# Re-pacing a convolution with a token search beside it: fewer search steps in one product stage, more in the last stage, and the input blocks dealt out anew

## The chip, the cores and the metric

One core of one Trainium2 chip runs the whole program. The metric is the device time of one launch in microseconds (us), the median of three runs. TensorE is called PE here, VectorE DVE, ScalarE ACT, GpSimd POOL and SyncE SP, as in the profile.

## The reference, cut to what matters

```python
def _attn_ref(x, h):                       # x (8, 6336, 128), h (6336, 128)
    L = 2 * S
    Yf = np.fft.rfft(x, n=L, axis=1) * np.fft.rfft(h, n=L, axis=0)[None]
    return np.fft.irfft(Yf, n=L, axis=1)[:, :S, :]

def _moe_ref(x, w_gate, w1, w2, capacity): # capacity 128, w1 (128, 1024), w2 (1024, 128)
    scores = np.einsum('bsd,d->bs', x, w_gate)
    out = x.copy()
    for b in range(B):
        top_idx = np.argpartition(-scores[b], capacity)[:capacity]
        xe = x[b, top_idx]
        ye = np.maximum(xe @ w1, 0.0) @ w2
        g = 1.0 / (1.0 + np.exp(-scores[b, top_idx]))
        out[b, top_idx] = x[b, top_idx] + g[:, None] * ye
    return out
```

A long causal convolution along the sequence, for 8 batches and 128 channels, and then, per batch, the 128 tokens with the highest score pass through a small two-layer network, whose result is added to them.

## The kernel before, in words

The convolution is a Fourier transform of length 6336 = 99 x 64, cut into matrix products. Batches go in pairs: group g handles batches 2g and 2g+1 (`xb[0]` and `xb[1]`, called the first and the second input), and there are four groups. Before group 0 the filter h takes the same way once. A group has these stages, all written out by one Python program whose order is the order on every engine's queue:

- `stage_a` (line 143), the first transform. A block is 8 channels of one input. POOL turns the block (`turn`, line 137, tile `xt`, three buffers; a block's turn is issued two blocks ahead), PE multiplies it with the table `fa` (line 156), and ACT or DVE empties the PSUM bank into `yp` (lines 59 and 61). A block has two steps; a step is 8 products, which are 16 records in the trace. A group has 32 blocks: for each half u of the channels (u = 0, 1) eight of the first and eight of the second input. Here `blocks(i, u)` stands for the eight blocks of input i in half u.
- `stage_b` (line 189), the product with the filter's spectrum for one half u of the channels, in 25 chunks of frequencies. Per chunk SP loads a table `w` (256 KB, four buffers, so four chunks ahead) and a spectrum piece `hr` (256 KB, seven ahead), PE makes the second transform (line 198), ACT writes a negated and swapped copy into a second bank (lines 201 and 202), DVE multiplies twice (line 206), and POOL, or in the first half DVE for each fifth chunk, adds (line 213).
- `stage_c` (line 217), the first inverse transform of one half, 32 steps of PE and an emptying each, written to `zp`.
- `stage_d` (line 227), the last stage, 32 steps. Per step PE makes four products (line 239, 8 records in the trace), ACT copies to `hr` (line 243, four places in rotation), ACT's queue stores to the output, POOL multiplies by the gate weights (line 247, tile `tm`), DVE sums them to scores (line 249).

Beside the stages of group g runs the *side*, the selection and the network for the pair before (`moe`, line 429). It is a Python generator whose steps are dealt out between steps of the stages by `mix` (line 439): a rate of 0.4 means that after each main step 0.4 is owed, and a side step is issued whenever a whole one is owed. Its steps: 1 starts the keys, 4 to 11 and 12 to 19 are two searches for the threshold, each of eight comparisons (DVE compares and counts, lines 278 and 281; in the next step PE sums over the partitions, line 284, and DVE makes the next thresholds, lines 285 to 292); 20 to 28 turn the winners into row numbers (step 27 makes the `lane` tiles of the second batch on DVE, lines 353 and 355, and step 28 multiplies them on PE, lines 361 and 363); 29 issues two gathers on POOL (line 385); 32 to 36 and 37 to 41 are the network of the first and of the second batch (`feed`, line 391), each ended by a scatter on POOL (line 422) that waits for DVE's line 421; the last scatter is in step 42. The side of the last pair follows the last stage with nothing beside it.

In groups 1 to 3 `stage_a` is split: `part` (20 blocks, 40 steps) runs alone with the side, `more` (12 blocks) runs beside the first half's `stage_b`, one step after each chunk. The second half's `stage_b` then starts with four chunks alone, and after that the first half's `stage_c` is mixed in at 1.33 steps a chunk. `zp` lies over part of `xb[1]` and of `yp`, so that the second input of the next pair can be loaded only when the last stage has read `zp`; its load is issued behind the last stage (line 512), that of the first input at the start of the second half's `stage_c` (line 501).

Of the kernel before, what the change touches and what calls it, by code (L numbers as in the profile page):

```python
# [32 lines left out]
def conv_moe(ctx, tc, x, h, w_gate, w1, w2, fa_d, wb_d, wc_d, at_d, tri_d, cst_d, out):  # L33
# [10 lines left out]
    def bank():  # L44
        return pp_.tile([128, 512], F32, tag="p", name="p")
# [4 lines left out]
    def product(out, table, moving, start=True, stop=True):  # L50

        n = out.shape[0]
        for a in range(0, n, 64):
            b = min(a + 64, n)
            nc.tensor.matmul(out[a:b], table[:, a:b], moving, start=start, stop=stop)  # L55

    def empty(act, dst, src):
        if act:
            nc.scalar.copy(out=dst, in_=src)  # L59
        else:  # L60
            v.tensor_copy(out=dst, in_=src)  # L61
# [13 lines left out]
    def load_x(src, half, parts=range(0, N2, 16)):  # L75
        s = src.rearrange("(a c) d -> a c d", c=N2)
        for n0 in parts:
            nc.sync.dma_start(out=xb[half][:, n0:n0 + 16], in_=s[:, n0:n0 + 16])
# [25 lines left out]
    def ahead(key, only=None):  # L104

        i = tables.index(key)
        while loaded[0] < len(tables) and loaded[0] <= i + AHEAD:
            item = tables[loaded[0]]
            if only and item[1] != key[1]:
                break  # L110
            loaded[0] += 1
            wt = tp.tile([128, 512], F32, tag="w", name="w", bufs=AHEAD + 1)
            if item[0] == "at":
                have[item] = wt[0:N1, 0:4 * N1].rearrange("p (m c n) -> p m c n", m=2, c=2)
                nc.sync.dma_start(out=have[item], in_=at_d[:, item[2]:item[2] + 2])
                continue
            k0, kn = kchunks[item[3]]
            have[item] = wt.rearrange("p (k c) -> p k c", c=128)
            nc.sync.dma_start(out=have[item][:, 0:kn], in_=wb_d[:, k0:k0 + kn])
        if key not in spectra:  # L120
            return
        i = spectra.index(key)
        while loaded[1] < len(spectra) and loaded[1] <= i + DEEP:
            item = spectra[loaded[1]]
            if item[1] != key[1]:
                break
            ht = hr[:, loaded[1] % 8 * 512:loaded[1] % 8 * 512 + 512].rearrange("p (t k d) -> p t k d", t=2, d=HD)
            loaded[1] += 1
            k0, kn = kchunks[item[3]]
            nc.sync.dma_start(out=ht[:, :, 0:kn], in_=hd[:, item[2], item[3], :, 0:kn])  # L130
            have["h", item] = ht
# [5 lines left out]
    def turn(block):  # L137
        half, d0, _ = block
        xt = tp.tile([N1, 8, N2], F32, tag="xt", name="xt", bufs=3)
        nc.gpsimd.tensor_copy(out=xt.rearrange("p d n -> p n d"), in_=xb[half][:, :, d0:d0 + 8])  # L140
        turned[block] = xt

    def stage_a(blocks, acts, lead=()):


        todo = list(blocks) + list(lead)
        for i, block in enumerate(blocks):
            for b in todo[i:i + 3]:
                if b not in turned:
                    turn(b)  # L150
            xt = turned[block]
            for q in range(2):
                pt = bank()
                for j in range(4):
                    for c in range(2):
                        nc.tensor.matmul(pt[c * 64:(c + 1) * 64, j * N1:(j + 1) * N1], xt[:, q * 4 + j],  # L156
                                         fa[:, c * N1:(c + 1) * N1], start=True, stop=True)
                p0 = (block[2] + q * 4) // 2
                empty(acts[(2 * i + q) % len(acts)], yp[:, p0:p0 + 2].rearrange("p j k t -> p j t k"),
                      pt[:, 0:4 * N1].rearrange("p (j t k) -> p j t k", j=2, t=2))  # L160
                if q:
                    del turned[block]
                yield

    def row(k, c0, n):
        return yp[:, c0 // 2:(c0 + n) // 2, k]
# [22 lines left out]
    def stage_b(g, u, adds):  # L189

        c0 = u * D
        for ci, (k0, kn) in enumerate(kchunks):
            key = ("b", g, u, ci)
            ahead(key)
            wt, ht = have.pop(key), have.pop(("h", key))
            pt = bank()
            for j in range(kn):
                product(pt[:, j * D:(j + 1) * D], wt[:, j], row(k0 + j, c0, D))
            pv = pt[:, 0:kn * D].rearrange("p (k b) -> p k b", b=D)
            pw = bank()[:, 0:kn * D].rearrange("p (k b) -> p k b", b=D)  # L200
            nc.scalar.mul(out=pw[0:64], in_=pv[64:128], mul=-1.0)  # L201
            nc.scalar.copy(out=pw[64:128], in_=pv[0:64])  # L202
            yv = yp[:, c0 // 2:(c0 + D) // 2, k0:k0 + kn].rearrange("p j k t -> p k j t")

            def times(dst, src, t):
                v.tensor_tensor(out=dst, in0=src.rearrange("p k (b j t) -> p k b j t", b=2, t=2),  # L206
                                in1=ht[:, t, 0:kn].rearrange("p k (j t) -> p k j t", t=2).unsqueeze(2).broadcast_to(
                                    [128, kn, 2, HD // 2, 2]), op=ALU.mult)

            times(yv.rearrange("p k (b j) t -> p k b j t", b=2), pv, 0)  # L210
            tx = tp.tile([128, KC, D], F32, tag="t", name="tx", bufs=3)[:, 0:kn]
            times(tx.rearrange("p k (b j t) -> p k b j t", b=2, t=2), pw, 1)
            (v if adds[ci % len(adds)] else nc.gpsimd).tensor_tensor(  # L213
                out=yv, in0=yv, in1=tx.rearrange("p k (j t) -> p k j t", t=2), op=ALU.add)
            yield

    def stage_c(u, acts):

        for j0 in range(u * D, u * D + D, 4):
            pt = bank()  # L220
            for i in range(4):
                product(pt[0:N1, i * 128:(i + 1) * 128], yp[:, (j0 + i) // 2, :, i % 2], wc)
            empty(acts[j0 // 4 % len(acts)], zp[:, j0 // 2:j0 // 2 + 2].rearrange("p j m t -> p j t m"),
                  pt[0:N1].rearrange("p (j t m) -> p j t m", j=2, t=2))
            yield
# [213 lines left out]
    def mix(main, *others):  # L439


        owed = [0.0] * len(others)
        for _ in main:
            for i, (it, rate) in enumerate(others):
                owed[i] += rate
                while owed[i] >= 1:
                    owed[i] -= 1
                    next(it, None)

    def rest(it):  # L450
        for _ in it:
            pass

    def blocks(half, u, lo=0, hi=8):
        return [(half, u * HD + i * 8, u * D + half * HD + i * 8) for i in range(lo, hi)]
# [14 lines left out]
    hs, a = stage_h(), stage_a(blocks(0, 0), (1, 0), blocks(1, 0)[0:2])  # L470
# [7 lines left out]
    side = iter(())  # L478
    for g in range(G):
        last = g == G - 1  # L480
        if g:
            part = blocks(0, 0) + blocks(0, 1, 0, 4) + blocks(1, 0)
            more = blocks(0, 1, 4) + blocks(1, 1)
            mix(stage_a(part, (1,), more[0:2]), (side, 0.45 if last else 0.25))
        else:
            more = blocks(0, 1) + blocks(1, 1)
        a = stage_a(more, (1, 1, 1, 0))
        mix(stage_b(g, 0, (0, 0, 0, 0, 1)), (a, 2 * len(more) / 24))
        rest(a)
        b, c = stage_b(g, 1, (0,)), stage_c(0, (1, 1, 0))  # L490
        for _ in range(4):
            next(b)
        mix(b, (c, 1.33), (side, 0.4))
        rest(c)
        if not last:
            if g == 0:
                nc.sync.dma_start(out=w1s, in_=w1)
                nc.sync.dma_start(out=w2s, in_=w2.rearrange("(c p) d -> p c d", p=128))
                v.tensor_copy(out=upper16, in_=upper)
                v.tensor_copy(out=lane16, in_=cst[:, 0:1])  # L500
            load_x(x[2 * g + 2], 0)
        mix(stage_c(1, (1,)), (side, 0.36))
        ss = mp.tile([N1, 2, N2], F32, tag="sc", name="sc", bufs=2)
        d = stage_d(g, ss)
        mix(itertools.islice(d, 24), (side, 0.35))
        if not last:
            for bl in blocks(0, 0)[0:2]:
                turn(bl)
        mix(d, (side, 0.35))
        rest(side)  # L510
        if not last:
            load_x(x[2 * g + 3], 1)
            ahead(("b", g + 1, 0, 0))
        side = moe(2 * g, 2, ss, shared)
        next(side)
# [56 lines left out]
```

## Time and profile before

| | us |
|---|---|
| median of three runs | 1062.93 |
| the three runs | 1063.11, 1054.4, 1062.93 |
| the profiled execution | 1058.81 |
| its span in the trace | 1057.0 |
| mean granted TensorE clock | 0.96 of full speed |

Times in the trace count from the start of the span. A stage's share is read by the time at which PE begins it: group 0 multiplies the first half from 110.2, group 1 starts at 296.2, group 2 at 529.1, group 3 at 758.0; PE ends the last stage of group 3 near 992 and the span ends at 1057.0.

### The profile page before, as it was taken

Reading aid. Unit: us, or ns where it says so; the run is one execution under the profiler, and the core shown is the slowest. Engines: PE = TensorE matmul, PEld = TensorE weight load, DVE = VectorE, ACT = ScalarE, POOL = GpSimd, SP = SyncE. Lnnn points to the kernel's source line nnn. Section 1 sums busy time; section 2 is a strip of 40 time slices with the busy share of each in tenths; the row PEclk is TensorE's granted clock in tenths of the full one; section 3 lists DMA queues with packets and bytes.
Section 4 is the critical chain, followed back from the end, with each engine's and each line's share of the span. In section 5 each row is a group of like instructions: output and inputs, shape, how many; then the busy total and the mean of one; then the engine's idle time right before and its main releaser. Section 6 shows DMA issues by size and latency. Waiting matters only on the chain.

```text
span 1057.0 us, 33223 instructions
## 1 busy us (share of the span) xinstructions
PE 933.4 (88%) x13756; PEld 851.5 (81%) x13756; DVE 629.8 (60%) x1225; ACT 593.7 (56%) x1071; POOL 569.0 (54%) x472
## 2 busy tenths in 40 slices
PE   2968999999989988999999899999989999999505
PEld 2968989997779988987799888977778899977404
DVE  0467687703365989524368999323577998123573
ACT  1456787773356876653368776643447777643101
POOL 2504796605866965226777765046856865046401
PEclk9988999999998999999999999999989999999856
DMA  8798888625674986416576875246645984036300
GB/s 275 260 341 305 260 279 267 203 118 155 211 236 135 322 291 189 143 50 197 169 244 223 291 256 172 93 119 180 207 150 180 305 292 132 7 116 190 113 1 10
DMA packets 117003, 203.17 MB, mean 192 GB/s; under 512 B 11303, under 2 KB 54538, under 8 KB 113290
## 3 DMA queue, kind: packets, MB, share of 16 engines
q1 hardware_dynamic: 89590, 174.05, 50.6%
q10 hardware_dynamic: 26752, 25.96, 7.5%
q8 instruction: 109, 1.79, 0.7%
q0 software_dynamic: 512, 1.05, 0.4%
q14 instruction: 40, 0.33, 0.1%
HBM read 161.56 MB, written 39.45 MB: 190 GB/s over the span
## 4 chain that ended last, share of the span: by engine, by line
PE 62%; DVE 13%; DMA 9%; POOL 5%; issue 5%; ACT 4%; SPq 1%; POOLq 0%; DVEq 0%; ACTq 0%
PE p L55 30%; PE p L239 16%; PE p L156 12%; POOL tm L247 3%; DVE tx L206 2%; DMA w<-tab_wb 2%; DVE cmp L278 2%; DVE slots L206 2%; DMA hr<-hd 2%; DVE num L281 2%; DMA slots<-in_h 1%; DMA out<-hr 1%; DMA hd<-hr 1%; ACT p L201 1%; DVE thr L292 1%
## 5 line engine op out<-in xcount | busy, mean ns | idle before, releaser
L59 ACT COPY slots<-p 128x396 f32<-128x396 f32 (+1 forms) x446 | 261.4, 587 | 148.0 <-PE p L156 78.1
L213 POOL TENSOR_TENSOR slots<-slots,tx 128x512 f32<-128x512 f32 x180 | 233.1, 1311 | 123.8 <-DVE tx L206 82.0
L156 PE MATMUL p<-fa,xt 99*64 99x99 f32 x4608 | 235.7, 256 | 32.5 <-POOL xt L140 23.3
L156 PEld LDWEIGHTS p<-fa,xt 99*64 99x64 f32 x4608 | 220.6, 141 | 38.0 <-POOL xt L140 26.3
L55 PE MATMUL p<-wc,slots 128*64 128x128 f32 (+1 forms) x4096 | 243.6, 273 | 5.4 <-DVE tx L206 2.2
L55 PE MATMUL p<-slots,w 128*64 128x128 f32 x3168 | 221.2, 279 | 15.2 <-ACT p L202 4.0
L55 PEld LDWEIGHTS p<-wc,slots 128*64 128x64 f32 (+1 forms) x4096 | 226.3, 126 | 10.0 <-DVE tx L206 3.6
L239 PE MATMUL p<-slots,w 99*99 99x256 f32 x1024 | 225.6, 377 | 2.9 <-ACT slots L59 2.9
L247 POOL TENSOR_TENSOR tm<-hr,wg 99x512 f32<-99x512 f32 x128 | 161.9, 1273 | 113.6 <-ACT hr L243 110.8
L140 POOL COPY xt<-slots 99x512 f32<-99x512 f32 x144 | 166.0, 1175 | 105.5 <-PE p L156 65.3
L239 PEld LDWEIGHTS p<-slots,w 99*99 99x99 f32 x1024 | 165.6, 163 | 57.0 <-ACT slots L59 3.8
L249 DVE TENSOR_REDUCE sc<-tm 99x4 f32<-99x512 f32 x128 | 87.9, 686 | 199.1 <-POOL tm L247 199.1
L55 PEld LDWEIGHTS p<-slots,w 128*64 128x64 f32 x3168 | 187.1, 136 | 19.5 <-ACT p L202 7.6
L206 DVE TENSOR_TENSOR slots<-p,hr 128x512 f32<-128x512 f32 (+1 forms) x200 | 136.1, 681 | 46.1 <-ACT p L202 45.7
L243 ACT COPY hr<-p 99x512 f32<-99x512 f32 x128 | 75.0, 586 | 139.0 <-PE p L239 125.9
L201 ACT ACTIVATE p<-p 64x512 f32<-64x512 f32 (+1 forms) x200 | 113.1, 566 | 67.3 <-PE p L55 57.7
L206 DVE TENSOR_TENSOR tx<-p,hr 128x512 f32<-128x512 f32 (+1 forms) x200 | 135.0, 675 | 0.0
L202 ACT COPY p<-p 64x512 f32<-64x512 f32 (+1 forms) x200 | 110.8, 554 | 6.3
L61 DVE COPY slots<-p 128x396 f32<-128x396 f32 (+1 forms) x98 | 60.0, 615 | 42.5 <-PE p L156 40.9
L385 POOL DMA_INDIRECT xe<-out,iu x8 | 8.0, 996 | 103.1 <-DVE cmp L353 88.3
L55 PE MATMUL m<-num,ones 99*35 99x6 bf16 (+1 forms) x128 | 14.1, 184 | 44.8 <-DVE num L281 44.7
L55 PEld LDWEIGHTS <-ones 99*35 99x35 bf16 (+1 forms) x128 | 8.9, 108 | 50.4 <-DVE num L281 42.6
(85 smaller groups left out, 453.5 us busy)
## 6 DMA issues: line engine op xcount, KB each, us to landing
w<-tab_wb SPq DMA_DIRECT2D x192, 256.0 KB
hr<-hd SPq DMA_DIRECT2D x192, 256.0 KB
slots<-in_x SPq DMA_DIRECT2D x32, 792.0 KB
out<-hr ACTq DMA_DIRECT2D x128, 198.0 KB
w<-tab_at SPq DMA_DIRECT2D x128, 153.1 KB
slots<-tab_wb SPq DMA_DIRECT2D x24, 256.0 KB
hd<-hr SPq DMA_DIRECT2D x24, 256.0 KB
slots<-in_h SPq DMA_DIRECT2D x4, 792.0 KB
```

The lines of the kernel that those rows point to most:

```text
L55: nc.tensor.matmul(out[a:b], table[:, a:b], moving, start=start, stop=stop)
L59: nc.scalar.copy(out=dst, in_=src)
L140: nc.gpsimd.tensor_copy(out=xt.rearrange("p d n -> p n d"), in_=xb[half][:, :, d0:d0 + 8])
L156: nc.tensor.matmul(pt[c * 64:(c + 1) * 64, j * N1:(j + 1) * N1], xt[:, q * 4 + j], fa[:, c * N1:(c + 1) * N1], start=True, stop=True)
L201: nc.scalar.mul(out=pw[0:64], in_=pv[64:128], mul=-1.0)
L202: nc.scalar.copy(out=pw[64:128], in_=pv[0:64])
L206: v.tensor_tensor(out=dst, in0=src.rearrange("p k (b j t) -> p k b j t", b=2, t=2), in1=ht[:, t, 0:kn].rearrange("p k (j t) -> p k j t", t ...
L213: (v if adds[ci % len(adds)] else nc.gpsimd).tensor_tensor(out=yv, in0=yv, in1=tx.rearrange("p k (j t) -> p k j t", t=2), op=ALU.add)
L239: nc.tensor.matmul(pt[0:N1, i * 2 * D:(i + 1) * 2 * D], at[:, i % 2, c], zp[:, :, c * N2 + m], start=(c == 0), stop=(c == 1))
L243: nc.scalar.copy(out=yt.rearrange("p b n (u d) -> p (n u) b d", u=2), in_=pt[0:N1].rearrange("p (n b d) -> p n b d", b=nb, d=HD))
L247: nc.gpsimd.tensor_tensor(out=tm, in0=hr[0:N1, o:o + 512].rearrange("p (c d) -> p c d", d=D), in1=wg[0:N1].unsqueeze(1).broadcast_to([N1, ...
L249: v.tensor_reduce(out=ss[:, :, m0:m0 + nd], in_=tm.rearrange("p (b n) d -> p b n d", b=nb), axis=AX.X, op=ALU.add)
```

## The change

```diff
-            part = blocks(0, 0) + blocks(0, 1, 0, 4) + blocks(1, 0)
-            more = blocks(0, 1, 4) + blocks(1, 1)
-            mix(stage_a(part, (1,), more[0:2]), (side, 0.45 if last else 0.25))
+            part = blocks(0, 0) + blocks(0, 1, 0, 6) + blocks(1, 0)
+            more = blocks(0, 1, 6) + blocks(1, 1)
+            mix(stage_a(part, (1,), more[0:2]), (side, 0.25))
...
-        mix(stage_b(g, 0, (0, 0, 0, 0, 1)), (a, 2 * len(more) / 24))
+        mix(stage_b(g, 0, (0, 0, 0, 0, 1)), (a, (2 * len(more) - 5.5) / 25))
         rest(a)
         b, c = stage_b(g, 1, (0,)), stage_c(0, (1, 1, 0))
-        for _ in range(4):
+        for _ in range(2):
             next(b)
-        mix(b, (c, 1.33), (side, 0.4))
+        mix(b, (c, 1.3), (side, 0.15))
...
-        mix(itertools.islice(d, 24), (side, 0.35))
+        mix(itertools.islice(d, 24), (side, 0.5))
...
-        mix(d, (side, 0.35))
+        mix(d, (side, 0.5))
```

By the rates, the side of groups 1 and 2 was at step 11 after `part`, 19 after the second half's `stage_b`, 30 after the second `stage_c`, 40 in the last stage, and two steps were left for behind it. Now it is at 12, 15, 26 and 42. In group 3 it was at 19 after `part` and ended in the middle of the last stage; now it goes as in the others. `part` has 44 steps instead of 40, `more` 20 instead of 24, of which 14 lie between the 25 chunks and 6 behind them. In group 0, 26 of the 32 steps of `more` lie between the chunks and 6 behind them.

PE's queue in the last stage of group 1, before (line 239 is the stage, 12 products are three of its steps; 396, 411 and 419 are the network of the pair before):

```order
L55 MATMUL p<-wc,slots 35x128
L239 MATMUL p<-slots,w 99x256 x36
L396 MATMUL p<-tri,xe 128x128
L239 MATMUL p<-slots,w 99x256 x12
L411 MATMUL p<-xet,w1s 128x128 x4
L239 MATMUL p<-slots,w 99x256 x12
```

The same place now:

```order
L55 MATMUL p<-wc,slots 35x128
L239 MATMUL p<-slots,w 99x256 x16
L361 LDWEIGHTS cmp
L361 MATMUL m<-lane_86,cmp 128x1
L361 LDWEIGHTS cmp
L361 MATMUL m<-lane_86,cmp 128x1
L363 LDWEIGHTS cmp
L363 MATMUL m<-hf,cmp 128x64
L363 LDWEIGHTS cmp
L363 MATMUL m<-hf,cmp 128x64
L239 MATMUL p<-slots,w 99x256 x40
L396 MATMUL p<-tri,xe 128x128
```

Side step 28 now stands behind the fourth step of the last stage, and the network begins behind the fourteenth step instead of the ninth.

DVE's queue at the same place now (249 is the last stage's sum, one per step; 367 to 376 end the first batch's row numbers, 353 and 355 write the `cmp` tiles that PE's line 361 loads):

```order
L355 SCALAR_TENSOR_TENSOR cmp<-tri,first,cmp 99x128
L249 TENSOR_REDUCE sc<-tm 99x2x2 x2
L367 TENSOR_SCALAR hit<-m,cst 128x128
L369 TENSOR_TENSOR hit<-hit,tri 128x128
L372 TENSOR_REDUCE col<-hit 128x1
L373 TENSOR_SCALAR col<-m 128x1
L376 TENSOR_TENSOR iu<-col 128x1
L353 TENSOR_SCALAR cmp<-tri,last 99x128
L355 SCALAR_TENSOR_TENSOR cmp<-tri,first,cmp 99x128
L353 TENSOR_SCALAR cmp<-tri,last 99x128
L355 SCALAR_TENSOR_TENSOR cmp<-tri,first,cmp 99x128
L249 TENSOR_REDUCE sc<-tm 99x2x2 x4
```

Before, all of these stood ahead of the first L249; now nine of them stand behind the second.

POOL's queue in group 1 from the end of the first half's `stage_b` to the next group, before (140 is a block's turn, 213 the addition, 247 the last stage, 385 the gathers, 422 a scatter):

```order
L213 TENSOR_TENSOR slots<-slots,tx 128x4x64x2 x2
L140 COPY xt<-slots 99x64x8
L213 TENSOR_TENSOR slots<-slots,tx 128x4x64x2 x28
L213 TENSOR_TENSOR slots<-slots,tx 128x3x64x2
L385 DMA xe<-out,iu 128x128 x2
L247 TENSOR_TENSOR tm<-hr,wg 99x512 x21
L422 DMA out<-xe,iu 12672x128
L247 TENSOR_TENSOR tm<-hr,wg 99x512 x3
L140 COPY xt<-slots 99x64x8 x2
L247 TENSOR_TENSOR tm<-hr,wg 99x512 x8
L422 DMA out<-xe,iu 12672x128
L140 COPY xt<-slots 99x64x8 x20
```

The same place now:

```order
L140 COPY xt<-slots 99x64x8
L213 TENSOR_TENSOR slots<-slots,tx 128x4x64x2
L140 COPY xt<-slots 99x64x8
L213 TENSOR_TENSOR slots<-slots,tx 128x4x64x2 x24
L213 TENSOR_TENSOR slots<-slots,tx 128x3x64x2
L247 TENSOR_TENSOR tm<-hr,wg 99x512 x6
L385 DMA xe<-out,iu 128x128 x2
L247 TENSOR_TENSOR tm<-hr,wg 99x512 x16
L422 DMA out<-xe,iu 12672x128
L247 TENSOR_TENSOR tm<-hr,wg 99x512 x2
L140 COPY xt<-slots 99x64x8 x2
L247 TENSOR_TENSOR tm<-hr,wg 99x512 x8
```

The last two turns of the first half's `stage_b` now stand behind all but one, and behind all, of its additions (28 additions followed the last turn before, 25 now, and a second half alone has 25). The gathers moved from ahead of the last stage to behind its sixth step. The last scatter still stands behind the 32nd step and ahead of the next group's third turn.

## Rows read from the trace of the kernel before

**Rows 1.** Busy time by stretch: length, PE, PEld, DVE, ACT, POOL, PEclk, DMA share, GB/s.

```profile
159.50:240.60 81.10, 80.40 (x1420) 80.16 (x1420) 37.69 (x62) 61.58 (x104) 32.36 (x25) 0.98 0.57 189
296.20:332.70 36.50, 31.77 (x657) 30.83 (x656) 21.19 (x45) 22.04 (x41) 23.23 (x22) 0.91 0.56 181
332.70:375.10 42.40, 40.35 (x782) 39.48 (x782) 38.14 (x62) 36.36 (x68) 36.62 (x30) 1.00 0.88 287
375.10:466.10 91.00, 84.69 (x1456) 80.07 (x1456) 64.65 (x139) 61.56 (x104) 34.94 (x28) 1.00 0.52 168
466.10:529.10 63.00, 63.00 (x322) 49.22 (x322) 23.14 (x40) 22.01 (x44) 42.91 (x35) 1.00 0.59 173
529.10:559.50 30.40, 28.49 (x656) 27.89 (x655) 20.57 (x45) 21.39 (x40) 23.41 (x22) 1.00 0.61 210
559.50:603.40 43.90, 40.17 (x780) 39.24 (x781) 40.01 (x62) 36.46 (x68) 36.32 (x30) 1.00 0.84 277
603.40:694.80 91.40, 84.63 (x1457) 80.03 (x1457) 64.65 (x139) 61.47 (x104) 34.88 (x28) 1.00 0.50 167
758.00:800.60 42.60, 33.88 (x670) 31.56 (x668) 32.86 (x86) 21.12 (x40) 23.40 (x22) 0.92 0.42 150
800.60:843.60 43.00, 40.72 (x782) 39.36 (x783) 37.79 (x59) 36.45 (x68) 36.85 (x30) 1.00 0.87 282
843.60:932.20 88.60, 86.75 (x1476) 83.46 (x1476) 51.41 (x105) 63.04 (x110) 36.07 (x29) 1.00 0.43 137
932.20:992.00 59.80, 59.38 (x289) 45.42 (x290) 21.76 (x36) 20.19 (x38) 40.26 (x32) 1.00 0.60 179
```

**Rows 2.** The same view: a stretch inside group 1's `stage_a`, one behind group 0's border.

```profile
318.00:323.50 5.50, 5.50 (x68) 5.50 (x70) 0.00 (x0) 1.57 (x3) 2.86 (x3) 0.50 0.59 199
...
159.50:166.00 6.50, 6.50 (x86) 6.50 (x88) 3.26 (x6) 4.09 (x8) 1.85 (x2) 0.74 0.53 164
```

**Rows 3.** Timeline: start, length, engine, work, [idle before, what ended it]; `stage_a`, group 1.

```profile
316.62 3.15 POOL L140 COPY xt<-slots 99x512 f32<-99x512 f32 x3 [5.16 <-DMA hr<-hd]
...
317.94 5.55 PE L156 MATMUL p<-fa,xt 99*64 99x99 f32 x64 [2.20 <-POOL xt L140]
```

**Rows 4.** POOL's groups of instructions in group 1's first-half `stage_b`: count, busy, mean ns.

```profile
L213 POOL TENSOR_TENSOR slots<-slots,tx 128x512 f32<-128x512 f32 x20 | 26.4, 1344 | 6.5 <-DVE tx L206 5.8 <-PE p L55 0.7
```

**Rows 5.** Timeline at the border between the halves: group 1 (PE, then DVE), group 0.

```profile
372.47 0.90 PE L55 MATMUL p<-slots,w 128*64 128x128 f32 x12
375.09 2.97 PE L55 MATMUL p<-slots,w 128*64 128x128 f32 x48 [1.73 <-ACT p L202]
...
375.37 0.55 DVE L206 TENSOR_TENSOR tx<-p,hr 128x384 f32<-128x384 f32 x1
...
159.50 6.41 PE L55 MATMUL p<-slots,w 128*64 128x128 f32 x80 [2.91 <-issue]
```

**Rows 6.** Timeline: group 1's last stage begins (PE, DVE); side step 27, first, last instruction.

```profile
466.10 15.85 PE L239 MATMUL p<-slots,w 99*99 99x256 f32 x72 [0.71 <-ACT slots L59]
...
471.88 0.69 DVE L249 TENSOR_REDUCE sc<-tm 99x4 f32<-99x512 f32 x1 [1.04 <-POOL tm L247]
...
454.44 0.35 DVE L367 TENSOR_SCALAR hit<-m,cst 128x128 f32<-128x128 f32 x1 [3.29 <-PE m L363]
...
456.54 0.35 DVE L355 SCALAR_TENSOR_TENSOR cmp<-tri,first,cmp 99x128 bf16<-99x128 f32 x1
```

**Rows 7.** All of line 292 on DVE: duration ns least/median/most.

```profile
L292 DVE TENSOR_TENSOR thr<-ge,cst x56: 166/168/1241, 309.3 to 1027.6; 99x6 f32<-99x6 f32 x56
```

**Rows 8.** Timeline: group 1's last stage ends, group 2 begins (PE, POOL, PE).

```profile
523.80 3.64 PE L239 MATMUL p<-slots,w 99*99 99x256 f32 x16
...
531.74 5.36 POOL L140 COPY xt<-slots 99x512 f32<-99x512 f32 x5
...
529.15 2.96 PE L156 MATMUL p<-fa,xt 99*64 99x99 f32 x64
532.88 2.36 PE L156 MATMUL p<-fa,xt 99*64 99x99 f32 x50 [0.77 <-POOL xt L140]
```

## Prediction

> **What bounds the kernel now.** I read the busy time by stretch first, cut where PE passes from one stage to the next [rows 1]. The reader is to see that PE is busy for nearly all of every stretch except the first transform of groups 1 and 3 (31.77 of 36.5 us, 33.88 of 42.6), and that three stretches are much longer than their twins. The second half's products with all of `stage_c` took 81.1 us in group 0, where no side runs, and 91.0, 91.4 and 88.6 in the other groups. DVE is why: 37.69 us busy in group 0's stretch, 64.65 in groups 1 and 2. The first half's `stage_b` is the other kind: in 42.4 us PE is busy for 40.35, DVE for 38.14, POOL for 36.62, ACT for 36.36, and the DMA share is 0.88. There nothing has much room, so work taken from PE there need not come back as time. The last stage is PE alone: 63.0 of 63.0.
>
> Then I read the clock in short stretches [rows 2], and the timeline around the waits [rows 3, 5, 6 and 8]. After PE had waited 2.20 us for a turned block in group 1, the granted clock was 0.50 for 5.5 us [rows 2, 3], the lower of its two levels (1.2 GHz): 2.75 us lost. After the 2.91 us wait at group 0's border it was 0.74 over 6.5 us [rows 2, 5]: 1.7 lost. Waits of 1.73 and 0.77 were followed by no such stretch [rows 1, 5, 8]. I price a new wait of 2 to 3 us with 1.0 more for the clock, between 0 and 2.75, and below the middle because the smaller waits cost nothing.
>
> **First transform (`part`).** Four more steps at group 2's pace, (30.4 - 0.8 of waiting) / 40 = 0.74 us each [rows 1, 8]: +3.0 in each of groups 1 to 3; the four steps leave the next stage.
> - Group 1: POOL's first turn of the second input started at 316.62, when its load had landed, and PE waited 2.20 for it and then ran at half clock [rows 2, 3]. PE now reaches that block 3.0 later, so wait and slow stretch go: 3.0 - 2.2 - 2.75 = -2.0. If the slow stretch stays, it is +0.8; if it falls on a later wait, up to +3.0.
> - Group 2: the third turned block is what is late. It stands on POOL behind the last scatter, which waits for DVE's line 421, itself behind the last sum. From the end of the last stage (523.80 + 3.64 = 527.44) to the end of that turn (a fifth of 5.36 after 531.74, 532.8) it is 5.4 us [rows 8]. Before, the network's last products filled 1.7 of these, then PE made two blocks in 2.96 and waited 0.77. Now those products stand two steps earlier, PE begins the blocks at once, and waits 5.4 - 2.96 = 2.4: +1.7, and +1.0 for the clock. With the four steps +5.7 (between +3.0 and +7.5).
> - Group 3 is then as group 2, 30.4 + 5.7 = 36.1, instead of 42.6 with 17 side steps at 0.45: -6.5.
> Together -2.8.
>
> **First half's products.** PE's own work between first and last chunk falls from 25 chunks and 24 steps to 25 and 14, that is from 40.45 us (332.7 to 372.47 + 0.70) [rows 1, 5] by 10 x 0.74 to about 33. It doesn't get that: DVE's 38.14 falls only by three emptyings, about as long as a product's 0.55, to 36.5, it begins some 2.5 after PE (an estimate: a chunk on PE and two copies on ACT come first), and it ends 2.8 after PE (375.37 + 0.55 against 373.15) [rows 1, 5], so PE's last chunk ends at 36.2 or later; POOL's 20 additions are 26.4 [rows 4] and its 10 turns the rest of 36.62, so with 7 turns 33.5; the loads of the whole stretch (42.4 x 287 GB/s = 12.2 MB) [rows 1] would run at 331 GB/s in 36.8 us. I take 36.8, near DVE's bound; the ends are 33 and 40.45. Behind it stand six steps, 4.4 us. The eighth block's turn now waits on POOL for the last additions but one and the ninth's for the last. The last of these waits for DVE's products of the chunk before the last, which end some 1.4 (two products) ahead of the last chunk's, so 1.4 behind PE. At 1.3 an addition [rows 4] and 1.1 a turn [rows 8] POOL ends the two turns about 2.3 and 4.8 after it. PE needs them after 1.5 and 3.9: two waits of some 1.0 each. Then 0.8 for emptying the last step (a 0.55 copy and the way to it, an estimate): the second half begins 7.0 behind the last chunk (before: 375.09 - 373.15 = 1.94). So 43.8 against 42.4, 43.9 and 43.0: +2.1 over groups 1 to 3, between -9 and +13. In group 0 PE sets the pace still; its wait of 2.91 and the slow 1.7 behind it become two waits of 2 and 0.8: -1.0, between -3 and +1.5. Together +1.1. `stage_c` with a lead of two chunks instead of four needs POOL's last addition some 6 us after it is done; the six steps cover that, and without them it would cost 2 chunks, 1.9.
>
> **Second half's products and `stage_c`.** Eight side steps fell to three beside these chunks (13 to 15, none waits for the one before it); comparisons 16 to 19 go to the second `stage_c`, where ACT does the emptying and DVE is free. The floor is group 0's stretch without its clock loss, 81.1 - 1.7 = 79.4 [rows 1, 2]. I add PE's share of the side, about 2.8 (an estimate: in group 0 PE was busy 80.40, in group 1 84.69 with the loss of 1.7 counted in the former, so 6.0 at most, and I take about half), and 1.3 of waits: 83.5, against 91.0, 91.4 and 88.6 [rows 1]: -7.5, -7.9, -5.1, together -20.5. Of group 3's 5.1, 3.2 is only the first batch's network going to the last stage. The ends are no gain but those 3.2, and -26.
>
> **Last stage.** Three things are added.
> - Step 28's products stand behind the stage's fourth step, and need tiles that DVE writes behind its second sum. That sum ends at 471.88 + 0.69 = 472.57; step 27 took 454.44 to 456.89 with POOL idle, 2.45, so they are ready at 475.0 at best. PE ends the fourth step at 466.10 + 4 x 15.85 / 9 = 473.15 [rows 6]. PE waits 1.9, with all later steps queued behind it, and the side is not what covers it, since PE has nothing else. POOL now multiplies meanwhile, which it didn't before: line 292 on DVE took 166 to 1241 ns [rows 7]; one such delay adds 1.1, two 2.2. I take one: 3.0 (1.9 to 4.1). The products are 0.2, the clock 1.0: 4.2 in each of groups 1 to 3, 12.6.
> - Group 3 takes over the first batch's network: 63.0 - 59.8 = 3.2 [rows 1].
> - The gathers stand behind POOL's sixth multiplication and hold it while DVE ends the row numbers, some 4 us (an estimate: a sum of 0.69, up to 2.45 for step 27's kind of work [rows 6], and the gathers themselves). POOL is busy for 42.91 of 63.0 [rows 1] and four places of `hr` lie between it and ACT, so nothing; without that room PE would lose about those 4.
> The last scatter's addition on DVE comes just ahead of the last pair's search: +0.3, an estimate from step 27's operations of 0.35. Together 16.1.
>
> The Trainium skill, SBUF — State Buffer, "SBUF: two separate sides", says that the port pair shared by VectorE and GpSimd is an exclusive lock, held for a whole instruction, which also a VectorE operation with two SBUF inputs takes. The trace agrees for line 292, from 166 to 1241 ns. By that rule lines 369, 376 and 355 of step 27 could each be held by a multiplication, and with two of them held the sum would be 3.3 us higher than mine.
>
> **Sum.** -2.8 + 1.1 - 20.5 + 16.1 = -6.1, on the profiled execution's 1058.8: 1052.7. Its span is 1057.0; the 1.8 around it stay. That execution is 4.1 below the median of three runs that lie 8.7 apart; I add about half the distance and forecast 1054.5.
>
> **Rivals.**
> - A, the covers hold. DVE's delay by POOL doesn't come (1.9 + 0.2 in the last stage and no slow clock, 2.1 x 3 = 6.3 less), no slow clock at the third turn (2.0 less), and PE's last chunk ends at 34.7, halfway to PE's own bound (2.1 x 3 = 6.3 less): 14.6 less, 1040. For it: gaps of 1.73 left the clock alone. Against: DVE's 38.14 of 42.4 [rows 1].
> - B, the loads set the first half's pace, the other side. At 287 GB/s and a share of 0.88 [rows 1] they may not run faster, because a table is asked for only when the chunk four before it is done. Then PE's last chunk stays at 40.45 and the six steps come on top: 3.65 x 3 = 11.0 more, 1065.5. It decides from a pace under about 340 GB/s downwards; above, DVE does. Against: group 1's fastest stretches.
> - C, the change doesn't do what it says: the 10 us in the second half are the border's backlog and DVE's products, not the comparisons. Then the 20.5 shrinks to the 3.2, and it is about 1072; with the waits of B nearer 1078. Against: the DVE columns of groups 0 and 1, 37.69 and 64.65.
>
> **How the numbers follow.** Forecast 0.50, A 0.28, B 0.14, C 0.08. The forecast's own range is 1047 to 1062. The range that leaves out 2 in 10 cuts A below its middle and the upper half of C: 1038 to 1071. Of the measured 1062.9, 1% is about what a measurement of this kernel can tell from no change: faster means under 1052.3, which is nearly all of A (0.26) and 0.15 of the forecast, 0.41; slower, over 1073.6, is half of C, some of B and a little besides, 0.10; the same is 0.49.
>
> **What would show it.** In the trace after: 83 to 84 us from the second half's first chunk to the last stage in groups 1 to 3 (wrong if near 91: C); a wait of 2 to 4 us on PE in front of line 361 behind four steps of the last stage, and about 2.4 in front of the third block of groups 2 and 3; two waits for turned blocks behind the 25th chunk; no wait for the second input in group 1. A first half shorter than 42 us speaks for A, longer than 46 for B. If the last stage is 63.5 instead of 67, the mechanism I price highest against the gain is not there.

## The result, and the profile after

The changed kernel takes 1070.43 us, the median of eight runs (1064.69 to 1077.31), against 1060.61 for the kernel before in eight runs beside them (1053.85 to 1063.11). The ratio is 1.0105 with a 95% interval of 1.0068 to 1.0142: slower by about 1%, where 1054.5 and a little faster was forecast. The profiled execution took 1064.69 with a span of 1062.9, the lowest of its eight, so the trace below holds 5.9 us of the loss and not the whole 9.8 between the medians. Ratios, here and below, compare all fast runs (one slow run, of the kernel with six steps behind, is left out), so they need not equal the ratio of two medians.

Busy time by stretch in the changed kernel, to be laid beside [rows 1] (length, PE, PEld, DVE, ACT, POOL, PEclk, DMA share, GB/s). `part`, first half, second half with `stage_c` and last stage of group 1, the first three of group 2, the first two of group 3:

```profile
295.60:332.50 36.90, 33.17 (x721) 32.37 (x720) 24.05 (x50) 24.18 (x45) 25.57 (x24) 0.95 0.57 180
332.50:379.00 46.50, 39.64 (x717) 36.61 (x718) 41.55 (x67) 35.03 (x65) 34.82 (x28) 1.00 0.84 282
379.00:462.20 83.20, 81.72 (x1451) 79.78 (x1451) 54.02 (x113) 61.42 (x104) 32.19 (x25) 1.00 0.53 171
462.20:530.40 68.20, 65.18 (x326) 50.13 (x326) 28.03 (x53) 21.31 (x43) 43.77 (x36) 0.97 0.54 158
530.40:564.80 34.40, 31.27 (x721) 30.72 (x720) 23.56 (x51) 24.34 (x45) 26.86 (x25) 1.00 0.60 194
564.80:613.10 48.30, 40.72 (x718) 37.92 (x718) 40.30 (x67) 35.06 (x65) 34.85 (x28) 0.96 0.82 271
613.10:697.80 84.70, 83.22 (x1451) 81.31 (x1451) 54.12 (x113) 61.49 (x104) 32.20 (x25) 0.98 0.51 167
766.00:800.20 34.20, 31.05 (x722) 30.70 (x722) 23.62 (x51) 24.31 (x45) 26.89 (x25) 1.00 0.57 195
800.20:846.10 45.90, 39.94 (x718) 36.73 (x719) 40.88 (x67) 35.05 (x65) 34.77 (x28) 1.00 0.86 285
```

The second half came out as wanted: 83.2, 84.7 and (846.1 to 929.2) 83.1 us instead of 91.0, 91.4 and 88.6, PE nearly always busy. Two things ate it. The first half has PE busy for less than before, 39.64 us instead of 40.35, and yet takes 46.5 instead of 42.4, with 48.3 (where the clock is 0.96) and 45.9 in the other groups. The last stage takes 68.2 instead of 63.0. `part` with its four more steps grew by 0.4 and 4.0 us in groups 1 and 2, and fell by 8.4 in group 3, where PE now idles for 3.2 us instead of 8.7.

Stage by stage, from the times at which PE begins each (us). The first column is all that precedes group 0's first half; the part behind the last stage is 65.4 in both:

| | before group 0 | group 0's halves | `part`, groups 1 to 3 | first half, 1 to 3 | second half and `stage_c`, 1 to 3 | last stage, 1 to 3 |
|---|---|---|---|---|---|---|
| before | 110.2 | 130.4 | 36.5, 30.4, 42.6 | 42.4, 43.9, 43.0 | 91.0, 91.4, 88.6 | 63.0, 63.0, 59.4 |
| after | 108.0 | 132.1 | 36.9, 34.4, 34.2 | 46.5, 48.3, 45.9 | 83.2, 84.7, 83.1 | 68.2, 68.2, 68.3 |
| sum of the differences | -2.2 | +1.7 | -4.0 | +11.4 | -20.0 | +19.3 |

The sum is +6.2, with the roundings, of the 5.9 by which the span grew. The -2.2 in front is not the change's: that stretch ended between 108.0 and 112.7 in the profiled executions, whose code for it is the same.

Timeline of group 1's first half in the changed kernel (start, length, work, [idle before it, what ended it]), at its waits, and the border to the second half, to be laid beside [rows 5]:

```profile
332.54 2.04 PE L55 MATMUL p<-slots,w 128*64 128x128 f32 x32 [0.59 <-ACT slots L59]
...
348.35 1.13 PE L55 MATMUL p<-slots,w 128*64 128x128 f32 x16 [1.25 <-DVE tx L206]
...
363.82 1.15 PE L55 MATMUL p<-slots,w 128*64 128x128 f32 x16 [0.64 <-DMA w<-tab_wb]
367.97 1.12 PE L55 MATMUL p<-slots,w 128*64 128x128 f32 x16 [1.40 <-DVE slots L206]
369.59 2.12 PE L55 MATMUL p<-slots,w 128*64 128x128 f32 x28
371.53 1.72 PE L156 MATMUL p<-fa,xt 99*64 99x99 f32 x36
376.69 1.59 PE L156 MATMUL p<-fa,xt 99*64 99x99 f32 x32 [0.92 <-POOL xt L140]
378.99 2.97 PE L55 MATMUL p<-slots,w 128*64 128x128 f32 x48 [0.71 <-issue]
```

PE ends the last chunk's products at 371.6, 39.1 us after it began the first (this stretch is called the loop below), and the six steps behind it, up to the second half's first chunk (the border), take 7.4 more. Before, the last chunk ended after 40.45 [rows 5]. So taking ten of 24 steps, 7.4 us of PE's work, out of the loop shortened it by 1.4 in group 1; in groups 2 and 3 the loop went from 42.0 to 39.4 and from 41.1 to 37.8.

Group 0 shows the other case: PE fills its loop, and DVE was busy for 36.33 of 45.5 us. The loop had 31 steps and has 26, 3.7 us of PE's work less, and became 3.7 shorter (before, then after):

```profile
110.20:155.70 45.50, 45.08 (x892) 44.04 (x894) 36.33 (x57) 38.28 (x72) 38.94 (x33) 1.00 0.83 264
```

```profile
108.00:149.80 41.80, 40.94 (x797) 39.98 (x799) 36.56 (x56) 35.43 (x67) 36.05 (x30) 1.00 0.91 298
```

PE's waits as sums, in the changed kernel's loop of group 1:

```profile
PE p L55 <- DMA w<-tab_wb: 1.9, 4, 0.6
PE p L55 <- DVE tx L206: 1.5, 2, 1.3
PE p L55 <- DVE slots L206: 1.4, 1, 1.4
```

In groups 2 and 3 the tables alone held PE for 4.1 and 2.7 us there. Before, PE waited in group 1's loop 0.8 us in all.

The last stage of group 1 in the changed kernel, timeline of PE, POOL and DVE around line 361; then the stretch behind it in the view by stretch:

```profile
462.19 7.18 PE L239 MATMUL p<-slots,w 99*99 99x256 f32 x32 [0.71 <-ACT slots L59]
...
467.96 0.69 DVE L249 TENSOR_REDUCE sc<-tm 99x4 f32<-99x512 f32 x1 [1.04 <-POOL tm L247]
468.39 1.27 POOL L247 TENSOR_TENSOR tm<-hr,wg 99x512 f32<-99x512 f32 x1 [0.46 <-DMA w<-tab_at]
...
468.94 0.87 DVE L369 TENSOR_TENSOR hit<-hit,tri 128x128 f32<-128x128 f32 x1
...
470.06 1.26 POOL L247 TENSOR_TENSOR tm<-hr,wg 99x512 f32<-99x512 f32 x1 [0.41 <-ACT hr L243]
470.22 1.12 DVE L376 TENSOR_TENSOR iu<-col 128x1 uint32<-128x1 f32 x1
...
471.98 0.18 PE L361 MATMUL m<-lane,cmp 99*128 99x1 bf16 x1 [2.61 <-DVE cmp L355]
...
472.56 0.18 PE L361 MATMUL m<-lane,cmp 99*128 99x1 bf16 x1 [0.41 <-DVE cmp L355]
```

```profile
472.00:480.00 8.00, 7.59 (x30) 5.42 (x31) 2.34 (x5) 1.33 (x3) 2.50 (x2) 0.79 0.32 97
```

PE waits 2.61 and 0.41 us for the tiles of side step 27. Behind the wait the granted clock was 0.79 over 8 us, which is 1.7 us of work lost. The wait has the same length in groups 2 and 3.

### The profile page after: what moved, and what is told of

It is laid out like the page before. It is cut to its first block, busy times and chain, and to the rows that moved or that the text cites. A ratio compares the mean times of both kernels' runs of the same rounds, so it can differ in the third digit from the quotient of the medians.

```text
span 1062.9 us, 33195 instructions
## 1 busy us (share of the span) xinstructions
PE 932.0 (88%) x13756; PEld 848.5 (80%) x13756; DVE 631.2 (59%) x1222; ACT 594.9 (56%) x1074; POOL 568.6 (53%) x472
## 3 DMA queue, kind: packets, MB, share of 16 engines
HBM read 161.56 MB, written 39.45 MB: 189 GB/s over the span
## 5 line engine op out<-in xcount | busy, mean ns | idle before, releaser
L156 PE MATMUL p<-fa,xt 99*64 99x99 f32 x4608 | 226.8, 254 | 39.2 <-POOL xt L140 31.2
L156 PEld LDWEIGHTS p<-fa,xt 99*64 99x64 f32 x4608 | 214.7, 140 | 45.3 <-POOL xt L140 33.6
L55 PE MATMUL p<-slots,w 128*64 128x128 f32 x3168 | 218.6, 278 | 19.7 <-DMA w<-tab_wb 9.2
L239 PE MATMUL p<-slots,w 99*99 99x256 f32 x1024 | 232.2, 384 | 2.8 <-ACT slots L59 2.8
L239 PEld LDWEIGHTS p<-slots,w 99*99 99x99 f32 x1024 | 168.0, 166 | 58.2 <-ACT slots L59 3.8
L249 DVE TENSOR_REDUCE sc<-tm 99x4 f32<-99x512 f32 x128 | 87.5, 686 | 204.2 <-POOL tm L247 204.2
L55 PE MATMUL m<-num,ones 99*64 99x6 bf16 (+1 forms) x128 | 16.4, 179 | 34.7 <-DVE num L281 34.4
L285 DVE TENSOR_SCALAR ge<-m 99x6 f32<-99x6 f32 x64 | 10.4, 162 | 51.5 <-PE m L55 51.5
L55 PEld LDWEIGHTS <-ones 99*64 99x64 bf16 (+1 forms) x128 | 10.8, 108 | 37.2 <-DVE num L281 30.8
```

The source lines that it names most:

```text
L239: nc.tensor.matmul(pt[0:N1, i * 2 * D:(i + 1) * 2 * D], at[:, i % 2, c], zp[:, :, c * N2 + m], start=(c == 0), stop=(c == 1))
L249: v.tensor_reduce(out=ss[:, :, m0:m0 + nd], in_=tm.rearrange("p (b n) d -> p b n d", b=nb), axis=AX.X, op=ALU.add)
```

## The experiments

Ratios are to the kernel before, run on the same chip beside each kernel, where its median was 1056.6, 1055.98 or 1056.16. The first four kernels ran on one chip, the next four on a second, the last on a third.

**The dealing of the blocks alone.** The changed kernel with the side's rates of before:

```diff
-            mix(stage_a(part, (1,), more[0:2]), (side, 0.25))
+            mix(stage_a(part, (1,), more[0:2]), (side, 0.45 if last else 0.25))
-        mix(b, (c, 1.3), (side, 0.15))
+        mix(b, (c, 1.3), (side, 0.4))
-        mix(itertools.islice(d, 24), (side, 0.5))
+        mix(itertools.islice(d, 24), (side, 0.35))
-        mix(d, (side, 0.5))
+        mix(d, (side, 0.35))
```

> The changed dealing of the blocks alone (22 blocks ahead, six steps behind the first half, lead of two chunks), with the side's rates of before. Waits theory (the trace of the changed kernel): the first half's products get 14 us longer over four groups as in the changed kernel, the four steps more cost 3 in groups 2 and 3 and 0 in group 1, and about 2 comes back at the second half's start: 1060.6 + 14 + 6 - 2, about 1078, slower than both. Rival (the dealing is good, the side's new pace costs the time): 1055 to 1060.

Measured: 1080.35, ratio 1.0222 (1.0154 to 1.0291). The dealing of blocks is the loss; the side's rates take back half of it.

**The side alone.** The kernel before with the side's new rates:

```diff
-            mix(stage_a(part, (1,), more[0:2]), (side, 0.45 if last else 0.25))
+            mix(stage_a(part, (1,), more[0:2]), (side, 0.25))
-        mix(b, (c, 1.33), (side, 0.4))
+        mix(b, (c, 1.33), (side, 0.15))
-        mix(itertools.islice(d, 24), (side, 0.35))
+        mix(itertools.islice(d, 24), (side, 0.5))
-        mix(d, (side, 0.35))
+        mix(d, (side, 0.5))
```

> The side's rates of the change alone, with the blocks of before. Waits theory: the second half's stretch falls by 20 over three groups, group 3's first transform by about 11, the last stage rises by 5 in each of groups 1 to 3 and 3 more in group 3 (line 361 waits 3 us behind the sixth step of the stage, half clock after it), the third turned block costs 2 in groups 2 and 3: 1060.6 - 20 - 11 + 18 + 4, about 1051. Rival (the side's new pace costs the time): 1065 or more.

Measured: 1046.12, ratio 0.9900 (0.9840 to 0.9959), faster by about 1%. The blocks' dealing costs 2.1% on top of it (1.0105 / 0.9900), and 2.2% without it: the two parts of the change add up and don't help each other.

**The row numbers ahead of the last stage.** One more comparison pair and step 27 go into the second `stage_c`, in the changed kernel and in the kernel with the side alone:

```diff
-        mix(stage_c(1, (1,)), (side, 0.36))
+        mix(stage_c(1, (1,)), (side, 0.42))
```

> The changed kernel with a rate of 0.42 instead of 0.36 in the second stage_c, so that side step 28 ends ahead of the last stage. Waits theory: no wait at line 361, the last stage back from 68.2 to about 63.3 in groups 1 to 3, at most 1 us each given back in stage_c: 1070.4 - 12, about 1058. Rival (the last stage is longer because the whole network now lies in it, and the wait at line 361 is only where that shows): 1068 to 1071.

> The side's rates of the change with the blocks of before, and 0.45 in the second stage_c, so that step 28 ends ahead of the last stage. Waits theory: as the run with the side's rates alone, less the 5 us of the last stage in three groups, and the third turned block in time since the side ends at the 28th step: about 1036, faster than both kernels. Rival: 1060 or more.

(0.45 in the second.) Measured: 1054.54, ratio 0.9987 (0.9954 to 1.0021), and 1037.91, ratio 0.9830 (0.9776 to 0.9885). All of line 361 in both kernels, ahead of the bar its busy time and mean, behind it PE's idle time before it; the first row is the kernel with the side alone, the second that with 0.45:

```profile
L361 PE MATMUL m<-lane,cmp 99*128 99x1 bf16 x16 | 2.4, 175 | 13.6 <-DVE cmp L355 13.6
```

```profile
L361 PE MATMUL m<-lane,cmp 99*128 99x1 bf16 x16 | 2.0, 174 | 4.6 <-DVE cmp L355 4.6
```

The last stage and the second half of group 1 in the kernel with 0.45:

```profile
373.36:459.88 86.52, 83.56 (x1456) 79.96 (x1456) 60.28 (x134) 61.39 (x104) 33.11 (x26) 1.00 0.53 175
459.88:522.90 63.02, 63.02 (x322) 49.09 (x322) 23.09 (x44) 21.41 (x43) 43.72 (x37) 1.00 0.58 172
```

The last stage is back at 63.0, with no idle time on PE, for 2.0 us more in the second half than with the side alone (84.5). 13.6 - 4.6 = 9.0 us of waits went, three times 3.0. This kernel beats both: 1.7% faster than the one before.

**Two more blocks ahead, none behind.** The changed kernel with all 20 steps of `more` between the chunks:

```diff
-        mix(stage_b(g, 0, (0, 0, 0, 0, 1)), (a, (2 * len(more) - 5.5) / 25))
+        mix(stage_b(g, 0, (0, 0, 0, 0, 1)), (a, 2 * len(more) / 24))
```

> The changed kernel with the remaining steps of the first transform dealt all between the chunks again (rate 20/24 in groups 1 to 3, 32/24 in group 0), none behind them; two more blocks ahead as in the change. If the six steps behind the border, with their waits for turned blocks, cost the time: the border falls from 7.4 to about 2.5 us with the last chunk where it is, 4.5 to 5 less in each of four groups, about 1052. Rival (the emptier loop itself runs no faster and the border is harmless): 1065 to 1071.

Measured: 1057.86, ratio 1.0005 (0.9971 to 1.0040). Between expectation and rival. Four steps fewer in the loop than before bring nothing there: in groups 1 to 3 its last chunk ends 40.6, 42.4 and 40.7 us after its first, and before it was 40.45, 42.0 and 41.1.

**Six steps behind, no block ahead.** The changed kernel with the 20 and 12 blocks of before, so 18 steps in the loop and six behind it:

```diff
-            part = blocks(0, 0) + blocks(0, 1, 0, 6) + blocks(1, 0)
-            more = blocks(0, 1, 6) + blocks(1, 1)
+            part = blocks(0, 0) + blocks(0, 1, 0, 4) + blocks(1, 0)
+            more = blocks(0, 1, 4) + blocks(1, 1)
```

> The changed kernel with the split of the blocks of before (20 ahead, 12 in the next stage, of which 18 steps between the chunks and 6 behind). If the loop of the first half is paced by DVE and the loads at some 39 us whatever PE has in it down to 14 steps: the loop stays at 39 with four steps more in it, and the four steps fall away ahead of it, 3 less in groups 2 and 3, 0 to 3 in group 1: about 1063. Rival (PE paces the loop): four steps in the loop cost what they gain ahead, 1070.

Measured: 1068.16, ratio 1.0083 (1.0038 to 1.0128), near the rival's time, but not by the rival's mechanism: the loop stayed at 39 as expected, and the border took the gain. The loop's end in group 1, then the border behind it (timeline; below it, both stretches):

```profile
375.47 2.25 PE L156 MATMUL p<-fa,xt 99*64 99x99 f32 x48
379.47 1.59 PE L156 MATMUL p<-fa,xt 99*64 99x99 f32 x32 [1.75 <-POOL xt L140]
381.91 2.91 PE L156 MATMUL p<-fa,xt 99*64 99x99 f32 x32 [0.85 <-POOL xt L140]
385.54 4.22 PE L55 MATMUL p<-slots,w 128*64 128x128 f32 x48 [0.72 <-issue]
```

```profile
370.00:378.00 8.00, 7.62 (x142) 6.99 (x140) 7.96 (x14) 6.79 (x14) 6.10 (x6) 1.00 0.94 314
378.00:385.50 7.50, 4.50 (x64) 4.00 (x64) 2.70 (x4) 1.57 (x3) 3.86 (x4) 0.73 0.40 136
```

With 18 steps the loop is 39.1 us (336.45 to 375.5), the same as with 14. The steps behind are paid whole, here 10.1 us with their waits and a clock of 0.73. While they run, DVE is busy for 2.70 of 7.5 us and the DMA share is 0.40.

Against the side alone (0.9900), the two blocks ahead cost 1.1%, the six steps behind 1.8%, and both 2.1%. All three have the lead of two chunks in the second half, which was not tried by itself.

**Half the loads of the spectrum, in groups 1 to 3.** The changed kernel; two lines go in, so line 206 is 207 here:

```diff
-            nc.sync.dma_start(out=ht[:, :, 0:kn], in_=hd[:, item[2], item[3], :, 0:kn])
+            tn = 1 if item[1] and item[2] == 0 else 2
+            nc.sync.dma_start(out=ht[:, 0:tn, 0:kn], in_=hd[:, item[2], item[3], 0:tn, 0:kn])
```

> The changed kernel, where groups 1 to 3 load only half of each spectrum piece in the first half (the other half of the tile keeps older numbers, so the result is another one): a quarter fewer bytes in that stage, all else the same. If the loads pace the loop: the waits for tables (2 to 4 us a group) go and it falls from 39 to about 37, near DVE's bound: 6 less, 1064. If DVE alone paces it: 1069 to 1071.

Measured: 1072.07, ratio 1.0136 (1.0100 to 1.0172). PE's waits in group 1's loop, as sums:

```profile
PE p L55 <- DVE slots L207: 2.3, 3, 1.0
PE p L157 <- DVE slots L207: 1.8, 3, 1.5
```

In group 1 no wait for a load is left, and waits for DVE stand in their place; in group 2 PE still waits 1.7 us for tables, and 1.9 for DVE. Group 1's loop is 37.8 us instead of 39.1, and the border behind it took that back: its stage is 47.5 instead of 46.5, and in groups 2 and 3 it is 46.0 and 46.0 instead of 48.3 and 45.9. The 1064 expected of loads that set the pace alone did not come.

**DVE's additions left out, in groups 1 to 3.**

```diff
+            if g and adds[ci % len(adds)]:
+                yield
+                continue
```

> The changed kernel without DVE's additions in the first half of groups 1 to 3 (each fifth chunk stays without its second product, so the result is another one): some 1.3 us less on DVE five times a group. If DVE paces the loop: it falls from 39 towards 36, held then by the loads, 2 to 3 less a group, about 1062. If the loads alone pace it: 1068 to 1071.

Measured: 1064.03, ratio 1.0085 (1.0050 to 1.0120), an interval that overlaps that of the changed kernel; by itself it settles nothing. PE's waits in group 1's loop:

```profile
PE p L55 <- DMA w<-tab_wb: 3.1, 5, 1.2
PE p L55 <- DVE tx L206: 1.5, 2, 1.0
```

Now the tables are what PE waits for most, and the loop is 38.8 us, in groups 2 and 3 36.9 and 38.3.

**Both cuts together.**

> The changed kernel with both of the last two cuts together in groups 1 to 3: the first half loads one half of each spectrum piece, and its additions on VectorE at every fifth chunk are left out (the output is another). In the changed kernel the loop of first transform, products and assembly takes 39.1 us up to its last chunk in group 1 with 14 steps on TensorE, about as long as with 18 or 20 steps. If VectorE and the loads both stand behind one another as its pace, taking one away shows the other (the two single cuts gave 47.5 and 45.4 us for the stage in group 1 against 46.5) and taking both away shortens the loop to about 35 us: the first half's stage of groups 1 to 3 falls from 45.9 to 48.3 to about 41 to 43 us each, and the time to about 1055 (1050 to 1060). If the pace is set by something else in the loop (ScalarE, GpSimd, the order of waits between them), the stage stays at 45 us or more and the time at 1063 to 1070.

Measured: 1055.66, ratio 0.9994 (0.9962 to 1.0026). Group 1's loop and the whole stage, in the changed kernel first, then with both cuts:

```profile
332.50:371.60 39.10, 34.08 (x606) 31.79 (x608) 36.77 (x60) 31.31 (x58) 29.87 (x24) 1.00 0.89 295
```

```profile
333.85:376.51 42.66, 38.84 (x716) 36.52 (x717) 35.00 (x62) 35.10 (x65) 33.52 (x28) 1.00 0.80 253
333.85:369.30 35.45, 33.45 (x606) 31.69 (x608) 31.63 (x56) 31.33 (x58) 28.66 (x24) 1.00 0.82 253
```

The loop falls to 35.4 us, of which PE is busy for 33.45, and the stage to 42.7, 42.0 and 42.5 us in groups 1 to 3. In group 1 one cut alone gave 1.3 or 0.3 us in the loop, both together 3.7; in the mean of three groups it is 1.1, 0.8 and 3.9. The unchanged loop took 37.8 to 40.4 us in the nine cases of the changed kernel, of the dealing alone and of the row numbers ahead. What one cut gives lies within that spread; what both give does not.

The loop, from the first chunk's begin to the end of the last chunk's products, in these kernels (us):

| | steps of `more` in the loop | group 1 | group 2 | group 3 |
|---|---|---|---|---|
| before | 24 | 40.45 | 42.0 | 41.1 |
| two blocks ahead, none behind | 20 | 40.6 | 42.4 | 40.7 |
| six steps behind, no block ahead | 18 | 39.1 | 39.3 | 39.1 |
| after | 14 | 39.1 | 39.4 | 37.8 |
| after, half the spectrum loads | 14 | 37.8 | 37.6 | 37.6 |
| after, no additions on DVE | 14 | 38.8 | 36.9 | 38.3 |
| after, both cuts | 14 | 35.4 | 34.5 | 34.7 |

## Why the prediction was wrong

The sum of the terms was -6.1 on the profiled execution, and it came out at +5.9. Of the 12.0 between, 9.3 are the first half's products, 3.2 the last stage and 2.7 group 0; the second half (+0.5), the first transform (-1.2) and the stretch before group 0 (-2.2) make up the rest, with the roundings. Between the forecast of 1054.5 and the median of 1070.43 lie 3.9 more, which no trace here explains: I put 1.8 between the profiled execution and the median, and it was 5.7.

**First half's products: this step failed.** I wrote that the last chunk would end at 36.8, "near DVE's bound": I took the bounds of PE, DVE, POOL and the loads one by one and let the longest set the loop. It ended at 39.1, 39.4 and 37.8 in groups 1 to 3, in sum 5.9 later, and the stage cost 11.4 more in these groups instead of 2.1. DVE and the loads hold the loop together, above the bound of either, as the last three experiments show. DVE did not fall in group 1's stage; it rose from 38.14 to 41.55. Its groups of instructions there, before, and in the same stage after:

```profile
L213 DVE TENSOR_TENSOR slots<-slots,tx 128x512 f32<-128x512 f32 x4 | 4.3, 1086 | 0.1
L61 DVE COPY slots<-p 128x396 f32<-128x396 f32 x6 | 3.4, 560 | 0.0
```

```profile
L213 DVE TENSOR_TENSOR slots<-slots,tx 128x512 f32<-128x512 f32 (+1 forms) x5 | 6.7, 1333 | 0.2
L61 DVE COPY slots<-p 128x396 f32<-128x396 f32 x5 | 2.8, 560 | 2.1 <-PE p L156 2.1
```

One emptying went from the stage, not three, because the six steps behind the loop are emptied in the same stage. A fifth addition fell inside it, and in this group each takes 1333 ns instead of 1086. The longer additions do not explain the loops, though: in those of groups 2 and 3 they took 873 and 1050 ns in the mean, less than the 1563 and 1284 of before. In the three loops DVE was busy for 36.8, 35.3 and 35.1 us, stood idle for 2.1, 3.8 and 2.5 in front of line 206, for which my bound had no term, and had done 22 or 23 of its 25 chunks when PE ended the last. The loads are the second bound.

Rival B (1065.5) had their place and the sign, and two of three stages passed the 46 us that were to speak for it. But it had the mechanism by half: with the loads halved PE waits mostly for DVE, without DVE's additions mostly for tables, and only with both gone is PE busy nearly throughout (33.45 of 35.45 us). The last three experiments show that; how DVE's delays and the tables' late requests work on one another within a chunk was not measured.

The border behind it was 7.4, 8.9 and 8.1 us instead of 7.0, in sum 3.4 longer. In group 1 it has one wait of 0.92 on POOL's turns instead of two of 1.0; groups 2 and 3 have both (0.49 and 0.94, 1.01 and 0.93). On the clock I had put nothing there, and in group 2 it was 0.78 from the border into the second half, which cost 1.8 of the 8.9 and 1.7 of the 84.7 behind:

```profile
604.20:620.00 15.80, 13.65 (x212) 12.99 (x210) 8.39 (x14) 8.15 (x16) 7.24 (x7) 0.78 0.49 160
```

Group 0 became 1.7 longer, where I had 1.0 shorter. PE does set its pace, as I wrote: the loop gave back all the work that was taken out. Its wait for a turned block is 2.16, near the 2 that I gave it. But a slow clock, 0.83 over the border's 10.2 us, costs the same 1.7 as before, where I had none left.

**Second half.** 83.2, 84.7 and 83.1 against 83.5: right, -20.0 against -20.5. That rules out rival C; that the time came near its 1072 is chance. The shorter lead of two chunks in `stage_c` cost nothing that the trace shows, and was not tried by itself.

**Last stage.** The wait before line 361 is 2.61 + 0.41 = 3.0, as forecast. The terms of it were nearly right too. The second sum ends 0.7 us before PE ends its fourth step, where I had 0.6, and the tiles are ready 3.85 after it (468.65 to 472.50), where I had 2.45 and one delay of 1.1. Two operations were delayed, line 369 by 0.58 and line 376 by 0.96 us (0.87 and 1.12 against the means of before, 0.29 and 0.16). The clock was under-priced: 1.0 was put down, the stretch lost 1.7 and with what lies around it 2.0, so the stage grew by 5.2 and 5.2 instead of 4.2. In group 3 the first batch's network is 63.0 - 59.4 = 3.6 and the rest again 5.3. Together +19.3 against +16.1. The two kernels with the row numbers made earlier show that waits and clock are all of it: without them the stage of groups 1 and 2 is 63.0 again in the first of these kernels, and 63.7 in group 3.

The Trainium skill, SBUF — State Buffer, "SBUF: two separate sides", says that the port pair shared by VectorE and GpSimd is an exclusive lock, which a VectorE operation with two SBUF inputs takes too. The trace agrees with the kinds of operation that it names, since line 369 ends 0.15 us behind a multiplication of POOL (469.81 and 469.66), and line 376 with the next (471.34 and 471.32). The price worked out from it, 3.3 us over mine, was too high: the two operations lost 1.5 in each group instead of 2.2, since the first of them began in the middle of a multiplication.

All of these two lines in the kernel before (count, busy us, mean ns):

```profile
L369 DVE TENSOR_TENSOR hit<-hit,tri 128x128 f32<-128x128 f32 x8 | 2.3, 292 | 0.3
L376 DVE TENSOR_TENSOR iu<-col 128x1 uint32<-128x1 f32 x8 | 1.3, 160 | 0.3
```

**First transform.** -4.0 against -2.8. In groups 2 and 3 the third block's wait is 2.55 and 2.56, where 2.4 was forecast, but no slow clock came behind it: that is 1.0 of the 1.7 and 1.9 us by which these groups are better than I had them, and the rest was not followed up. In group 1 the wait for the second input is gone, as forecast, yet the stage is 0.4 longer instead of 2.0 shorter, since the slow stretch only moved ("if it falls on a later wait", up to +3.0):

```profile
314.73 1.81 PE L156 MATMUL p<-fa,xt 99*64 99x99 f32 x32 [2.09 <-issue]
```

```profile
314.70:321.00 6.30, 6.27 (x111) 6.27 (x111) 2.20 (x6) 2.86 (x6) 2.32 (x3) 0.73 0.87 309
```

What PE waited for in those 2.09 us the trace doesn't name; it stays open.

## What to carry to other kernels

Before work is taken out of a loop, look for every engine and queue that is busy for nearly all of it: in group 1 PE (39.45 of 39.8 us), DVE (35.73) and the loads (a share of 0.88) stood so close that taking 7.4 us from PE shortened the loop by 1.4, and by 2.6 and 3.3 in the next two groups. In group 0, where DVE was busy for 36.33 of 45.5, 3.7 us taken out came back whole. What was taken out then stands behind the loop alone, at its full price and beside engines with little to do; work should leave a full loop only for a stage that has room. And a small chain between two engines (a search's last steps) belongs where neither is the bound, with its last link well ahead of the stage in which one engine alone sets the time: raising one rate from 0.36 to 0.42 or 0.45 was worth 1.2% on top of the changed kernel and 0.7% on top of the side alone, by the middles of their intervals.

## What was not expected of the hardware

- The length of a wait does not tell what the clock does behind it. In the border of group 2 waits of 0.49, 0.94 and 0.71 us went with 0.78 over 15.8 us (above), and in that of group 3 the longer ones of 1.01, 0.93 and 0.71 with full speed. After 2.09 us in group 1's `part` it was 0.73 over 6.3 us, and after 3.0 in the last stage 0.79 over 8; after 2.55 in group 2's `part` it stayed at full speed, the higher of the two levels (2.4 GHz):

```profile
535.92 4.29 PE L156 MATMUL p<-fa,xt 99*64 99x99 f32 x95 [2.55 <-POOL xt L140]
```

```profile
536.00:542.00 6.00, 6.00 (x142) 6.00 (x144) 4.80 (x7) 4.12 (x8) 5.39 (x6) 1.00 0.89 288
```

- The same addition on DVE, with the same count of four in group 1's loop, took 1086 ns in the mean in the kernel before, 1292 in the changed one, 1470 with two blocks ahead and none behind, and 1556 with the side alone. In the changed kernel each of these four begins while POOL's addition is under way and ends 0.54 to 0.56 us behind its end, so its length depends on how the two queues happen to lie.
- Two nearly full resources hide each other: in group 1 cutting either gained 1.3 or 0.3 us of a 39.1 us loop and cutting both 3.7, and over three groups 1.1 or 0.8 and 3.9 in the mean.
